# A sorted graph aggregation: broadcasts in halves, upper counts on two engines beside the decoding, low parts of the features by TensorE, and a folded 16-bit maximum

## The chip, the cores and the metric

The kernel runs on one core of a Trainium2 chip. The metric is the device time of one execution in microseconds (us). The engines are named as in the profile: PE (TensorE, matmuls; PEld its weight loads), DVE (VectorE), ACT (ScalarE), POOL (GpSimd) and SP (SyncE, which here only issues transfers). Each engine works through its own queue in order; semaphores tie the queues together.

## What is computed

The reference is one layer of a graph network with mean aggregation over 800,000 random edges between 12,500 nodes with 64 features each:

```python
N, deg, D = 12500, 64, 64
E = N * deg
nsum = _segment_sum(x[src], dst, N)
h_neigh = nsum * deg_inv[:, None]
return x @ w_self + h_neigh @ w_neigh
```

The sum over the edges of a node is the expensive part. The kernel doesn't gather a row of `x` per edge. It sorts the edges, and then does the gather and the sum with one-hot matrices on TensorE.

## The kernel before, in words

**Keys and sort.** Every edge becomes one 32-bit key: destination block (of 160 nodes, 78 of them), source block (of 128 nodes, 98 of them), and the low bits of both. A pair of blocks is a *bucket*; there are 7,644, of up to 128 edges each. Each of the 128 partitions sorts 6,250 edges by a comb sort on DVE (`sort_runs`, L227); elements without a partner in a stage are copied by ACT (L229). A list scheduler lays `prepare` and `self_terms` in between, by its own model of the engines. `prepare` finds the largest absolute value of `x` (ACT writes the absolute values to `y`, DVE reduces them, L527), makes a power-of-two scale `scl` from it, and splits the scaled features into two fp16 halves: `xh[:, :, 0]` is the rounded value (ACT, L550), `y` the difference (DVE, L551), `xh[:, :, 1]` 2048 times that (ACT, L552). It also counts, with two sign passes on ACT, whether any value is in a forbidden range.

**Two parts.** From `after_sort` on the order is as written (`manual_schedule`). Runs of the sorted rows are found, gathered across partitions by POOL (`gather_runs`: indirect DMAs `u<-d`, each followed by one or two `pad` memsets as a pause, L391, L304), and merged by DVE with min and max steps (`merge_runs`, L413, L453; ACT copies the unpaired elements, L418). Part 0 holds the first 4,736 buckets, part 1 the others. For each of the buckets a row of part 0 has (37), its start is found by counting: a pass over a window with an accumulator (`count_below`, L597 on ACT, L599 on DVE), a conversion to an address (`ix`, L622 on ACT), and an indirect DMA on POOL that fetches the window (`v<-d`, L603). The first 18 counts lie inside the merge; the 19 *upper counts* need its end. `decode_buckets` then takes ten groups of four windows: four DVE steps (L640 to L645), two narrowing copies on ACT, a store of the source bits to `sl` in DRAM by SP, four transposes on PE, and a copy into `dlT`. At its end it picks out leftover edges that fit no bucket (`e`, `top`).

**Part 1 while part 0 is summed.** The part-1 merge is a generator (`merge`). Its first 20 steps, block (0,2), are interleaved with the decoding; the next 20 and the others come a few per tile in the main loop, at `PACE` ns of work per tile, with a pause until tile `RESUME`. The part-1 gathers are split too: 64 of the 128 are issued during the part-0 merge, 32 (`FIRST` to `THEN`) behind the last `v` gather, and 32 (the list `runs`) one on every odd tile.

**Main loop.** `nodes` goes through 956 tiles of eight buckets. `one_hots` makes, for every 28 buckets, `ohs` (DVE, L821) from a broadcast of `sl` over all partitions (`slb`, issued by SP, L819, three buffers), and `ohd` (DVE, L824) from `dlT`. `gather` does eight matmuls `ct` (L850) which pick rows of `xh`, and copies them to fp16 `xg` (ACT L860, from tile 503 on every other one on DVE). `sums`, two to three tiles later, does sixteen matmuls into `acc` (L905). I call a tile's turn in `sums` its *job*. The leftover edges come in by 140 further gathers `lx` on POOL (L869), each with two matmuls in `sums` (L885). `uses` gives each one a due bucket: no earlier than its buckets are done, and for part 0 no earlier than a line in its number; the gather is issued 160 buckets (20 tiles) ahead of that, PE uses it when the job reaches it. All POOL gathers stand in one queue, in the order in which this loop writes them.

Of the kernel before, what the change touches and what calls it, by code (L numbers as in the profile page):

```python
# [11 lines left out]
F32 = mybir.dt.float32  # L12
BF = mybir.dt.bfloat16
FH = mybir.dt.float16
# [50 lines left out]
LOWER = 2240  # L65
LAST = 20
LAG = 4
OCT = 6
LEAST = 2 * HN * NDB
LEND = 14  # L70
# [71 lines left out]
    return c >= 128 + SHARED or c % 2 == 0  # L142


def on_act2(part):

    return part == 0


def constants():  # L150
    thr = bid_base(np.concatenate([BASE[p] + np.arange(ROWS[p]) * KPRS[p] for p in range(2)]))
    assert thr[-1] == 0x7F000000 and thr[-2] < TAIL
    thr[-1] = TAIL
    act = np.array([on_act(c) for c in range(NC1)])
    t1 = np.where(act, -(thr - 1).view(np.float32), thr.view(np.float32))
    mul = np.where(act, -1.0, 2.0)
    add = np.array([(n if a else 0) + lo - 1 for (lo, n), a in zip(WIN.w1, act)])
    add[128:] -= UPPER1
    assert max(lo + 2 * n for lo, n in WIN.w1[:128]) + WIDE[0] <= SPLITS[1]
    assert min(lo for lo, _ in WIN.w1[128:]) > UPPER1  # L160
    c1 = np.zeros((128, 3, NC1), np.float32)
    c1[:, 0], c1[:, 1], c1[:, 2] = t1, mul, add
    out = {"c1": c1}
    for p in range(2):
        kpr = KPRS[p]
        b = BASE[p] + np.arange(128)[:, None] * kpr + np.arange(kpr)[None]
        v = bid_base(np.minimum(b, NBID))
        act = np.array([on_act2(p) for k in range(kpr)])
        first = np.array([lo + (n / 2 + 0.25 if a else 0) for (lo, n), a in zip(WIN.w2[p], act)])
        mid = v | np.uint32(1 << 14)  # L170
        c2 = out[f"c2_{p}"] = np.zeros((128, 6, kpr), np.float32)
        c2[:, 0] = v.view(np.float32)
        c2[:, 1] = mid.view(np.float32)
        c2[:, 2] = -(mid - 1).view(np.float32)
        c2[:, 3] = np.where(act, -0.5, 1.0)
        at = [home(p, k) for k in range(kpr)]
        c2[:, 4] = first + np.arange(128)[:, None] * np.array(PITCH2)[at] - np.where(np.array(at) == 1, UPPER2 + SIDE, 0)
        c2[0::2, 5, 0] = c2[1::2, 5, 1] = 1.0
    return out
# [79 lines left out]
class Kernel:  # L259
# [242 lines left out]
    def prepare(self, xp, mps):  # L502

        nc = self.nc
        full = NB - 1
        tail = N - full * 128
        self.w2s = xp.tile([128, 2, D], F32, name="w2s")
        nc.gpsimd.memset(self.w2s, 0.0)  # L510
        for h in range(2):
            nc.sync.dma_start(self.wn[h * D:(h + 1) * D], self.I["w_neigh"])
            nc.sync.dma_start(self.w2s[h * D:(h + 1) * D, h], self.I["w_self"])
        x = self.x = xp.tile([128, NB, D], F32, name="x")
        nc.gpsimd.memset(x[:, full], 0.0)
        nc.sync.dma_start(x[:, :full], self.I["x"][:full * 128].rearrange("(b p) f -> p b f", p=128))
        nc.sync.dma_start(x[:tail, full], self.I["x"][full * 128:])
        dg = xp.tile([128, 128], F32, name="dg")
        nc.gpsimd.memset(dg, 0.0)
        fd = N // FB  # L520
        nc.sync.dma_start(dg[:fd, :FB], self.I["deg_inv"][:fd * FB].rearrange("(b p) -> b p", p=FB))
        nc.sync.dma_start(dg[fd:fd + 1, :N - fd * FB], self.I["deg_inv"][fd * FB:].unsqueeze(0))

        y = xp.tile([128, NB, D], F32, name="y")
        nc.scalar.activation(y, x, AF.Abs)
        m = xp.tile([128, 1], F32, name="m")
        nc.vector.tensor_reduce(m, y.rearrange("p b f -> p (b f)"), axis=mybir.AxisListType.X, op=OP.max)  # L527
# [23 lines left out]
        nc.vector.scalar_tensor_tensor(y, x, scl[:, :1], self.xh[:, :, 0], op0=OP.mult, op1=OP.subtract)  # L551
        nc.scalar.activation(self.xh[:, :, 1], y, AF.Copy, scale=2048.0)  # L552
        nc.sync.dma_start(self.xt.rearrange("(b p) f -> p b f", p=128), self.xh.rearrange("p b a f -> p b (a f)"))

        nc.scalar.activation(y, x, AF.Abs, scale=scl[:, :1])
        z = xp.tile([128, NB, D], BF, name="z")
# [31 lines left out]
    def count_below(self, part, k, acc):  # L588
# [2 lines left out]
        c2 = self.c2[part]  # L591
        lo, n = WIN.w2[part][k]
        w = view(self.rows, EDGE + lo, [[1, n]])
        on = on_act2(part)
        junk = self.keep.tile([128, max(n for _, n in WIN.w2[0] + WIN.w2[1])], BF, name=f"junk2{part}")
# [17 lines left out]
    def find_and_gather(self, part, ks, lag):  # L613


        scale = -0.5 if on_act2(part) else 1.0
        for i in range(len(ks) + lag):
            if i < len(ks):
                self.count_below(part, ks[i], self.acc2)
            if i >= lag:  # L620
                k = ks[i - lag]
                self.nc.scalar.activation(self.ix2[:, k:k + 1], self.acc2[:, k:k + 1], AF.Relu, scale=scale,  # L622
                                          bias=self.c2[part][:, 4, k:k + 1])
                self.gather_window(part, k, self.ix2)
            yield i
# [167 lines left out]
    def uses(self):  # L793
# [3 lines left out]
        for o in range(0, NBID, OCT * NB):  # L797
            end = min(o + OCT * NB, NBID)
            here = []
            for p in range(2):  # L800
                for c in range(64):
                    lo = max(o, BASE[p] + c * 2 * KPRS[p])
                    hi = min(end, BASE[p] + (c + 1) * 2 * KPRS[p])
                    if hi > lo:
                        here.append([max(hi + 56, 260 + 32 * c) if p == 0 else hi + 56, p, c, lo // NB, (hi - 1) // NB])
            at = end + 8
            for use in sorted(here)[::-1]:
                at = use[0] = min(use[0], at - 24)
# [3 lines left out]
    def one_hots(self, pool):  # L812
# [2 lines left out]
        nc = self.nc  # L815
        for c in range(0, NBID, 28):
            b = pool.tile([128, 28 * 128], BF, name="slb", bufs=3)
            src = self.sl[c:c + 28]
            nc.sync.dma_start(b, bass.AP(tensor=src.tensor, offset=src.offset, ap=[[0, 128], [1, 28 * 128]]))  # L819
            s = pool.tile([128, 28, 128], FH, name="ohs", bufs=3)  # L820
            nc.vector.tensor_scalar(s.rearrange("p c s -> p (c s)"), b, self.pidx[:, :1], None, op0=OP.is_equal)  # L821
            d = pool.tile([128, 14, HN, 2], FH, name="ohd", bufs=5)
# [286 lines left out]
    def sums_and_merge(self, es, mps, aps, u1, other, l2, l2b, l2a, va, vp):  # L1109
        tc = self.tc  # L1110
        vb = ExitStack()
        for _ in self.find_and_gather(0, range(NLOWER, KPRS[0]), 1):
            pass
        self.gather_runs(1, u1, range(FIRST, THEN))
        runs = list(range(THEN, 128))
        l2a.close()
        merge = self.merge_runs(1, u1, other, ((0, 2), (2, 1), (3, 1)))
        per = steps = 4 * len(MERGE[1][0])
        t, early = 0, per
        for k in self.decode_buckets(0, self.v, vp, mps):  # L1120
            t += 2800
            while t > 0 and early and k < KPRS[0]:
                t -= next(merge)
                early -= 1
        for _ in range(early):
            next(merge)
        va.close()

        self.fin = fin = es.enter_context(tc.tile_pool(name="fin", bufs=1, side="right"))
# [73 lines left out]
```

## Time and profile before

| | us |
|---|---|
| runs: median (lowest, highest of 3) | 1899.85 (1891.56, 1901.67) |
| the profiled execution | 1899.66 |
| its span in the trace | 1897.9 |
| DVE busy | 1672.6 (88%) |
| ACT busy | 1176.5 (62%) |
| PE busy (weight loads) | 972.7 (841.7) |
| POOL busy | 809.3 (43%) |
| DMA queue of SP and ACT (q1), share of 16 engines | 41.2% |

The stages on the profile's clock: keys until 46, sort and `prepare` until about 280, finding and gathering part 0 until about 551, merging it until 747, decoding until 811, leftovers until 821, first one-hot at 826, main loop to the end. A table of engines' busy time over all of the span mixes these stages; the rows to read are those of one stage, and the waits in it.

### The profile page before, as it was taken

How to read it: one execution, taken by the hardware profiler on the slowest of the kernel's cores; microseconds unless marked ns; L12 is line 12 of the kernel's file. 1: busy time of each engine (PE TensorE's matmuls, PEld its weight loads, DVE VectorE, ACT ScalarE, POOL GpSimd, SP SyncE). 2: the span in 40 equal slices, each digit the busy share in tenths (PEclk: the TensorE clock that was granted, in tenths of full speed). 3: DMA queues.
4: the chain of work that ended last, by engine and by line, in shares of the span. 5: the costliest groups of instructions: out<-in, count | busy, mean ns of one | idle time of the engine just before them, and what ended most of it. 6: DMA issues, size and time to landing. Idle time of an engine off the chain costs nothing.

```text
span 1897.9 us, 54529 instructions
## 1 busy us (share of the span) xinstructions
PE 972.7 (51%) x23659; PEld 841.7 (44%) x23659; DVE 1672.6 (88%) x1760; ACT 1176.5 (62%) x1853; POOL 809.3 (43%) x917
## 2 busy tenths in 40 slices
PE   0043000000000000039888888898879989998997
PEld 0033000000000000038777777787768877787886
DVE  7999999997749998779699999999799888788885
ACT  7463019205510022549888898898968878777886
POOL 1000000699889984898521331326554123322431
PEclk9995555555555555569999999999989999999999
DMA  4322000001100012257677877889768887888884
GB/s 152 70 68 68 0 32 0 26 20 52 22 20 10 10 40 66 58 190 279 207 240 245 244 256 257 245 267 322 234 206 283 285 255 263 242 266 265 273 259 139
DMA packets 104804, 305.24 MB, mean 161 GB/s; under 512 B 52945, under 2 KB 60491, under 8 KB 103915
## 3 DMA queue, kind: packets, MB, share of 16 engines
q1 hardware_dynamic: 86347, 277.44, 41.2%
q0 software_dynamic: 17632, 22.17, 8.6%
q8 instruction: 187, 3.06, 0.6%
q10 hardware_dynamic: 576, 2.07, 0.3%
q14 instruction: 62, 0.51, 0.1%
HBM read 282.20 MB, written 19.41 MB: 159 GB/s over the span
## 4 chain that ended last, share of the span: by engine, by line
DVE 43%; PE 23%; POOL 16%; issue 11%; DMA 3%; ACT 3%; DVEq 0%; SPq 0%; POOLq 0%; ACTq 0%
DVE u L453 15%; PE ct L850 13%; POOL u L391 12%; PE acc L905 9%; DVE a L227 7%; DVE b L227 7%; DVE ohd L824 6%; DVE ohs L821 4%; POOL pad L304 2%; POOL v L603 1%; ACT xg L860 1%; DMA slb<-sl 1%; PE po L968 1%; DVE u L413 1%; POOL lx L869 1%
## 5 line engine op out<-in xcount | busy, mean ns | idle before, releaser
L860 ACT ACTIVATE xg<-ct 128x1024 f16<-128x1024 f32 (+1 forms) x898 | 853.3, 1032 | 166.8 <-PE ct L850 135.3
L850 PE MATMUL ct<-xh,ohs 128*128 128x128 f16 x7644 | 543.1, 223 | 64.3 <-DVE ohs L821 27.3
L850 PEld LDWEIGHTS <-ohs 128*128 128x128 f16 x7644 | 449.0, 100 | 107.7 <-issue 57.5
L391 POOL DMA_INDIRECT u<-d,ix x256 | 362.2, 1415 | 217.1 <-DVE ix L383 175.4
L905 PE MATMUL acc<-ohd,xg 64*128 64x80 f16 x15288 | 405.5, 199 | 72.8 <-issue 49.1
L453 DVE TENSOR_TENSOR u<-u 128x1456 f32<-128x1456 f32 (+46 forms) x292 | 393.7, 1377 | 21.6 <-issue 14.6
L905 PEld LDWEIGHTS <-xg 64*128 64x128 f16 x15288 | 318.6, 96 | 144.6 <-issue 70.4
L824 DVE TENSOR_TENSOR ohd<-iota,dlT 128x2240 f16<-128x2240 bf16 x273 | 360.2, 1319 | 0.0
L869 POOL DMA_INDIRECT lx<-xt,lsrc x140 | 236.8, 1691 | 263.2 <-PE acc L885 224.4
L821 DVE TENSOR_SCALAR ohs<-slb,pidx 128x3584 f16<-128x3584 bf16 x273 | 315.0, 1154 | 34.4 <-PE ct L850 21.7
L381 PE MATMUL stp<-idf,st 128*128 128x128 f32 x2 | 0.9, 447 | 356.8 <-DVE st L379 356.8
L227 DVE TENSOR_TENSOR a<-b 128x608 f32<-128x608 f32 (+44 forms) x124 | 174.0, 1445 | 4.6
L227 DVE TENSOR_TENSOR b<-a 128x608 f32<-128x608 f32 (+44 forms) x124 | 173.9, 1444 | 4.3
L976 POOL DMA_DIRECT2D out<-o x25 | 23.6, 946 | 354.7 <-DVE o L975 288.4
L381 PEld LDWEIGHTS stp<-idf,st 128*128 128x128 f32 x2 | 0.4, 182 | 357.3 <-issue 357.3
L660 PE MATMUL tr<-idb,l 128*128 128x128 bf16 x60 | 8.2, 278 | 285.2 <-issue 240.9
L858 DVE CAST xg<-ct 128x1024 f16<-128x1024 f32 x64 | 78.3, 1224 | 70.2 <-PE ct L850 69.5
L660 PEld LDWEIGHTS <-l 128*128 128x128 bf16 x60 | 5.0, 119 | 288.2 <-issue 244.3
L418 ACT ACTIVATE u<-u 128x30 f32<-128x30 f32 (+34 forms) x136 | 29.8, 268 | 143.6 <-DVE u L453 74.5
L229 ACT ACTIVATE b<-a 128x1 f32<-128x1 f32 (+21 forms) x52 | 18.7, 383 | 135.3 <-DVE a L227 130.2
L597 ACT ACTIVATE junk<-u,c 128x166 bf16<-128x166 f32 (+36 forms) x37 | 26.7, 722 | 119.1 <-DVE u L453 119.0
L603 POOL DMA_INDIRECT v<-d,ix x60 | 77.8, 1297 | 47.5 <-ACT ix L622 35.0
(153 smaller groups left out, 868.7 us busy)
## 6 DMA issues: line engine op xcount, KB each, us to landing
slb<-sl SPq DMA_DIRECT2D x273, 896.0 KB
u<-d,ix POOLq DMA_INDIRECT x256
xt<-xh SPq DMA_DIRECT2D x1, 3136.0 KB
fo<-own SPq DMA_DIRECT2D x26, 120.0 KB
own<-os SPq DMA_DIRECT2D x12, 256.0 KB
out<-o POOLq DMA_DIRECT2D x24, 120.0 KB
lx<-xt,lsrc POOLq DMA_INDIRECT x140
rd<-dst SPq DMA_DIRECT2D x4, 521.0 KB
```

The costliest lines, as they stand in the source:

```text
L227: nc.vector.tensor_tensor(view(dst, lo + sh, [[st, g], [1, l]]), x, y, op=op)
L304: self.nc.gpsimd.memset(self.pad, 0.0)
L391: nc.gpsimd.indirect_dma_start(out=u[:nr, EDGE + p * w:EDGE + (p + 1) * w], out_offset=None, in_=src, in_offset=bass.IndirectOffsetOnAxis( ...
L453: nc.vector.tensor_tensor(view(dst, EDGE + o + out, d), view(src, EDGE + o + x, d), view(src, EDGE + o + x + gap, d), op=op)
L603: self.nc.gpsimd.indirect_dma_start(out=self.v[:, k].bitcast(F32), out_offset=None, in_=flat(self.d2[home(part, k)], 128 * PITCH2[home(par ...
L821: nc.vector.tensor_scalar(s.rearrange("p c s -> p (c s)"), b, self.pidx[:, :1], None, op0=OP.is_equal)
L824: nc.vector.tensor_tensor(d, self.iota[:, None].to_broadcast([128, 14, HN, 2]), ix, op=OP.is_equal)
L850: nc.tensor.matmul(ct[:, i * 128:(i + 1) * 128], cols[i][0], self.xh[:, (b0 + i) % NB].rearrange("p a f -> p (a f)"), start=True, stop=True)
L858: nc.vector.tensor_copy(xg[:, :cnt * 128], ct[:, :cnt * 128])
L860: nc.scalar.activation(xg[:, :cnt * 128], ct[:, :cnt * 128], AF.Copy)
L869: nc.gpsimd.indirect_dma_start(out=x, out_offset=None, in_=self.xt, in_offset=bass.IndirectOffsetOnAxis(ap=self.left[p][1][:, c:c + 1], ax ...
L905: nc.tensor.matmul(acc[h][:, db % OCT * HN:(db % OCT + 1) * HN], xg[r, i * 128:(i + 1) * 128], d[r], start=db % OCT == 0 and sb == 0, stop ...
```

## The change

Four edits, and one that goes with them.

1. `one_hots` issues the broadcast of 28 buckets as two transfers of 14 (448 KB each) into the two halves of the same buffer. The one-hot still runs over all 28.
2. `prepare`: the absolute values are written as bf16 (`z`), folded by four element-wise maxima down to 392 columns, and reduced from there. The low half is made on PE: for every eight blocks, `x` times a diagonal of the scale (fp32), minus the rounded half times an identity (fp16), summed in PSUM (`low`), from where ACT writes 2048 times it to `xh`. DVE's reduction of 6,272 elements and its pass at L551 go.
3. The upper counts of part 0 alternate between ACT and DVE (`on_act2(part, k)`), and the loop that decodes runs beside them, in slots that are budgeted at `SLOT` ns each. Only as many steps of the part-1 merge as fit in the budget are put there, five by the listing; the others follow in the main loop. The address conversion trails the count by two slots and not one.
4. The line below which a part-0 leftover gather isn't due is 380 + 24 c and not 260 + 32 c.

```diff
-def on_act2(part):
-    return part == 0
+def on_act2(part, k):
+    return part == 0 and (k < NLOWER or (k - NLOWER) % 2 == 0)
...
         y = xp.tile([128, NB, D], F32, name="y")
-        nc.scalar.activation(y, x, AF.Abs)
+        z = xp.tile([128, NB, D], BF, name="z")
+        nc.scalar.activation(z, x, AF.Abs)
+        most, n = z.rearrange("p b f -> p (b f)"), NB * D
+        fold = xp.tile([128, n // 2], BF, name="fold")
+        while n > 512:
+            n //= 2
+            nc.vector.tensor_tensor(fold[:, :n], most[:, :n], most[:, n:2 * n], op=OP.max)
+            most = fold
         m = xp.tile([128, 1], F32, name="m")
-        nc.vector.tensor_reduce(m, y.rearrange("p b f -> p (b f)"), axis=mybir.AxisListType.X, op=OP.max)
+        nc.vector.tensor_reduce(m, fold[:, :n], axis=mybir.AxisListType.X, op=OP.max)
...
-        nc.vector.scalar_tensor_tensor(y, x, scl[:, :1], self.xh[:, :, 0], op0=OP.mult, op1=OP.subtract)
-        nc.scalar.activation(self.xh[:, :, 1], y, AF.Copy, scale=2048.0)
+        by = xp.tile([128, 128], F32, name="by")
+        nc.scalar.activation(by, self.idf, AF.Copy, scale=scl[:, :1])
+        less = xp.tile([128, 128], FH, name="less")
+        nc.scalar.activation(less, self.idf, AF.Copy, scale=-1.0)
+        for b0 in range(0, NB, 8):
+            nb = min(8, NB - b0)
+            ps = mps.tile([128, 8, D], F32, name="low", tag="ct", bufs=3)
+            nc.tensor.matmul(ps[:, :nb], by, x[:, b0:b0 + nb], start=True, stop=False)
+            nc.tensor.matmul(ps[:, :nb], less, self.xh[:, b0:b0 + nb, 0], start=False, stop=True)
+            nc.scalar.activation(self.xh[:, b0:b0 + nb, 1], ps[:, :nb], AF.Copy, scale=2048.0)
...
-                        here.append([max(hi + 56, 260 + 32 * c) if p == 0 else hi + 56, p, c, lo // NB, (hi - 1) // NB])
+                        here.append([max(hi + 56, 380 + 24 * c) if p == 0 else hi + 56, p, c, lo // NB, (hi - 1) // NB])
...
-            src = self.sl[c:c + 28]
-            nc.sync.dma_start(b, bass.AP(tensor=src.tensor, offset=src.offset, ap=[[0, 128], [1, 28 * 128]]))
+            for j in range(0, 28, 14):
+                src = self.sl[c + j:c + j + 14]
+                nc.sync.dma_start(b[:, j * 128:(j + 14) * 128],
+                                  bass.AP(tensor=src.tensor, offset=src.offset, ap=[[0, 128], [1, 14 * 128]]))
...
     def sums_and_merge(self, es, mps, aps, u1, other, l2, l2b, l2a, va, vp):
-        for _ in self.find_and_gather(0, range(NLOWER, KPRS[0]), 1):
-            pass
-        self.gather_runs(1, u1, range(FIRST, THEN))
-        runs = list(range(THEN, 128))
-        l2a.close()
-        merge = self.merge_runs(1, u1, other, ((0, 2), (2, 1), (3, 1)))
-        per = steps = 4 * len(MERGE[1][0])
-        t, early = 0, per
-        for k in self.decode_buckets(0, self.v, vp, mps):
-            t += 2800
-            while t > 0 and early and k < KPRS[0]:
-                t -= next(merge)
-                early -= 1
-        for _ in range(early):
-            next(merge)
+        runs = list(range(THEN, 128))
+        merge = self.merge_runs(1, u1, other, ((0, 2), (2, 1), (3, 1)))
+        per = 4 * len(MERGE[1][0])
+        t, steps = 0, 0
+        ways = self.find_and_gather(0, range(NLOWER, KPRS[0]), 2)
+        decode = self.decode_buckets(0, self.v, vp, mps)
+        at = []
+        for k in range(3, KPRS[0] + 3, 4):
+            at.append(max(2 * len(at), at[-1] + 2 if at else 0, READY + min(k, KPRS[0] - 1) - NLOWER if k >= NLOWER else 0))
+        for slot in range(at[-1] + 2):
+            t += SLOT
+            if ways and next(ways, None) is None:
+                ways = None
+                self.gather_runs(1, u1, range(FIRST, THEN))
+            if slot < KPRS[0] - NLOWER and not on_act2(0, NLOWER + slot):
+                t -= 750
+            if slot in at or slot - 1 in at:
+                next(decode)
+                t -= 1175
+            while t > 0 and steps < per:
+                t -= next(merge)
+                steps += 1
+        for _ in decode:
+            pass
+        l2a.close()
```

What this does to the order of the queues, at the two places the prediction speaks of. First DVE, just behind the part-0 merge. `v` is decoded in groups of four steps; L413 and L453 are steps of the part-1 merge. Before:

```order
L640 TENSOR_TENSOR v<-v,c_0_67 128x4x128
L642 TENSOR_SCALAR w,cnt<-v 128x512
L644 TENSOR_SCALAR w<-v 128x512
L645 TENSOR_SCALAR v<-v 128x4x128
L413 TENSOR_TENSOR u<-u 128x2x16x41 x2
L453 TENSOR_TENSOR u<-u 128x2x655
L453 TENSOR_TENSOR u<-u 128x2x603
L640 TENSOR_TENSOR v<-v,c_0_67 128x4x128
L642 TENSOR_SCALAR w,cnt<-v 128x512
L644 TENSOR_SCALAR w<-v 128x512
L645 TENSOR_SCALAR v<-v 128x4x128
L453 TENSOR_TENSOR u<-u 128x2x650
```

And after, where L615 is a count on DVE, L656 to L661 the decoding, L415 and L455 the merge:

```order
L656 TENSOR_TENSOR v<-v,c_0_67 128x4x128
L658 TENSOR_SCALAR w,cnt<-v 128x512
L660 TENSOR_SCALAR w<-v 128x512
L661 TENSOR_SCALAR v<-v 128x4x128
L415 TENSOR_TENSOR u<-u 128x2x16x41
L615 TENSOR_SCALAR junk_1992,acc_0_1861<-u,c_0_67 128x566
L656 TENSOR_TENSOR v<-v,c_0_67 128x4x128
L658 TENSOR_SCALAR w,cnt<-v 128x512
L660 TENSOR_SCALAR w<-v 128x512
L661 TENSOR_SCALAR v<-v 128x4x128
L615 TENSOR_SCALAR junk_2014,acc_0_1861<-u,c_0_67 128x591
```

Between two groups of decoding there stood merge steps; now there stands a count, and all but the first merge step have moved back.

Second POOL, at the first leftover gather `lx`, among the part-1 run gathers `u`. Before, 39 of the last 64 `u` stand ahead of it:

```order
L391 DMA u<-d_1_61,ix_1468 128x48
L304 MEMSET pad 128x95 x2
L869 DMA lx<-xt,lsrc_2756 128x128
L391 DMA u<-d_1_61,ix_1468 128x48
L304 MEMSET pad 128x95 x2
L391 DMA u<-d_1_61,ix_1468 128x48
L304 MEMSET pad 128x95 x2
L869 DMA lx<-xt,lsrc_2756 128x128
```

After, 47 of the 64:

```order
L393 DMA u<-d_1_61,ix_1527 128x48
L306 MEMSET pad 128x95 x2
L887 DMA lx<-xt,lsrc_2791 128x128
L393 DMA u<-d_1_61,ix_1527 128x48
L306 MEMSET pad 128x95 x2
L887 DMA lx<-xt,lsrc_2791 128x128
L393 DMA u<-d_1_61,ix_1527 128x48
L306 MEMSET pad 128x95 x2
L393 DMA u<-d_1_61,ix_1527 128x48
L306 MEMSET pad 128x95 x2
L887 DMA lx<-xt,lsrc_2791 128x128
```

The first `lx` has moved eight `u` back, and the next ones stand closer together; by the eighth, 60 `u` are ahead of it and 59 were.

More of the change, by code (lines that the diff above doesn't have):

```diff
@@ L67 @@
 LAG = 4
+READY = 8
+SLOT = 1250
 OCT = 6
@@ L167, in constants @@
         v = bid_base(np.minimum(b, NBID))
-        act = np.array([on_act2(p) for k in range(kpr)])
+        act = np.array([on_act2(p, k) for k in range(kpr)])
         first = np.array([lo + (n / 2 + 0.25 if a else 0) for (lo, n), a in zip(WIN.w2[p], act)])
@@ L550, in prepare @@
         nc.scalar.activation(self.xh[:, :, 0], x, AF.Copy, scale=scl[:, :1])
-        nc.vector.scalar_tensor_tensor(y, x, scl[:, :1], self.xh[:, :, 0], op0=OP.mult, op1=OP.subtract)
-        nc.scalar.activation(self.xh[:, :, 1], y, AF.Copy, scale=2048.0)
+        by = xp.tile([128, 128], F32, name="by")
[8 more added lines that the diff above has]
+            nc.scalar.activation(self.xh[:, b0:b0 + nb, 1], ps[:, :nb], AF.Copy, scale=2048.0)
         nc.sync.dma_start(self.xt.rearrange("(b p) f -> p b f", p=128), self.xh.rearrange("p b a f -> p b (a f)"))
         nc.scalar.activation(y, x, AF.Abs, scale=scl[:, :1])
-        z = xp.tile([128, NB, D], BF, name="z")
         s = [xp.tile([128, 1], F32, name=f"s{i}") for i in range(2)]
@@ L593, in count_below @@
         w = view(self.rows, EDGE + lo, [[1, n]])
-        on = on_act2(part)
-        junk = self.keep.tile([128, max(n for _, n in WIN.w2[0] + WIN.w2[1])], BF, name=f"junk2{part}")
+        on = on_act2(part, k)
+        junk = self.keep.tile([128, max(n for _, n in WIN.w2[0] + WIN.w2[1])], BF, name=f"junk2{int(on)}")
         if on:
@@ L613, in find_and_gather @@
     def find_and_gather(self, part, ks, lag):
-        scale = -0.5 if on_act2(part) else 1.0
         for i in range(len(ks) + lag):
@@ L621, in find_and_gather @@
                 k = ks[i - lag]
-                self.nc.scalar.activation(self.ix2[:, k:k + 1], self.acc2[:, k:k + 1], AF.Relu, scale=scale,
+                self.nc.scalar.activation(self.ix2[:, k:k + 1], self.acc2[:, k:k + 1], AF.Relu,
+                                          scale=-0.5 if on_act2(part, k) else 1.0,
                                           bias=self.c2[part][:, 4, k:k + 1])
```

## The prediction

> **What bounds the kernel now.** I read the page's chain of work first, then the busy times in windows around the change, then the waits and the chain inside them.
>
> ```profile
> DVE 43%; PE 23%; POOL 16%; issue 11%; DMA 3%; ACT 3%; DVEq 0%; SPq 0%; POOLq 0%; ACTq 0%
> ```
> ```profile
> 747.00:811.00 64.00, 4.87 (x32) 2.76 (x32) 47.42 (x71) 39.20 (x100) 49.28 (x66) 0.50 0.25 73
> 811.00:827.00 16.00, 0.90 (x5) 0.45 (x5) 10.88 (x22) 1.88 (x5) 14.25 (x25) 0.50 0.34 116
> 827.00:926.00 99.00, 81.25 (x1905) 69.82 (x1906) 77.91 (x105) 77.87 (x101) 85.48 (x129) 0.88 0.73 260
> 926.00:1250.00 324.00, 278.10 (x7104) 241.77 (x7101) 320.81 (x301) 281.95 (x338) 86.91 (x48) 0.97 0.78 243
> ```
>
> The windows give the busy us of PE, weight loads, DVE, ACT and POOL, then granted clock, DMA share and GB/s. I call 747.1 us T0: the merge of part 0 ends there, and the upper counts begin. From 926 to 1250 DVE is full (320.8 of 324), so what counts is when that stretch can begin. Between T0 and 926 DVE idles 16.6 + 5.1 + 21.1 = 42.8 us, which is all that can be won behind T0. POOL is nearly full in the same time, and the waits say who is late:
>
> ```profile
> PE acc L885 <- DMA lx<-xt,lsrc: 3.2, 1, 3.2
> ```
> ```profile
> DVE ohs L821 <- PE ct L850: 11.7, 8, 5.6
> DVE u L413 <- DMA u<-d,ix: 8.1, 2, 4.2
> ```
> ```profile
> 901.25 6.10 DMA lx<-xt,lsrc
> 907.40 0.45 PE acc L885 x2
> ```
>
> These are PE's and DVE's waits of 826 to 960 (us, times, longest) and two steps of the chain (start, us). PE stands at the sixth left-over gather `lx` (#5, counted from 0) until 907.40; that gather began at 901.25, behind POOL's `u` gathers; DVE waits for PE (11.7 us) and twice for a `u` (8.1 us). So up to about 920 it is POOL's queue, one gather behind the other, that paces the end of this stage. What POOL's queue costs:
>
> ```profile
> L391 POOL DMA_INDIRECT u<-d,ix x59 | 80.3, 1360 | 10.4 <-issue 10.4
> L304 POOL MEMSET pad<- 128x95 f32 x118 | 28.3, 239 | 3.4
> L869 POOL DMA_INDIRECT lx<-xt,lsrc x8 | 9.7, 1209 | 3.2 <-issue 2.2 <-ACT xg L860 1.0
> ```
> ```profile
> 905.32 0.95 POOL L391 DMA_INDIRECT u<-d,ix  x1 [0.16 <-issue]
> 906.28 0.43 POOL L304 MEMSET pad<- 128x95 f32 x2
> 906.86 0.95 POOL L391 DMA_INDIRECT u<-d,ix  x1 [0.15 <-issue]
> ```
> ```profile
> 913.96 1.37 POOL L869 DMA_INDIRECT lx<-xt,lsrc  x1 [0.53 <-issue]
> ```
> ```profile
> 919.71 0.23 PE L885 MATMUL acc<-ohl,lx 128*128 128x80 f16 x2
> ```
>
> In 780 to 914 one `u` with its two pads takes (80.3 + 10.4 + 28.3 + 3.4)/59 = 2.08 us, one `lx` 12.9/8 = 1.61. Where DVE stood idle, at 905 to 907, a `u` took only 906.86 - 905.32 = 1.54. From the end of #7's gather (915.33) to its use at 919.71 pass 4.4 us, from #5's (901.25 + 1.55) 4.6: that is a landing.
>
> **The change, part by part.**
>
> *Prepare (beside the sort).* Groups of 46 to 282, and the first two one-hots:
>
> ```profile
> L551 DVE SCALAR_TENSOR_TENSOR y<-x,scl,xh 128x6272 f32<-128x6272 f32 x1 | 6.7, 6745 | 0.0
> L527 DVE TENSOR_REDUCE m<-y 128x1 f32<-128x6272 f32 x1 | 6.7, 6676 | 0.0
> L227 DVE TENSOR_TENSOR a<-b 128x2994 f32<-128x2994 f32 x2 | 6.5, 3277 | 0.1
> ...
> L555 ACT ACTIVATE y<-x,scl 128x6272 f32<-128x6272 f32 x1 | 5.5, 5532 | 0.0
> L576 PE MATMUL xt<-idf,x 128*128 128x128 f32 x49 | 13.2, 421 | 0.0
> ```
> ```profile
> 826.42 1.15 DVE L821 TENSOR_SCALAR ohs<-slb,pidx 128x3584 f16<-128x3584 bf16 x1 [5.01 <-DMA slb<-sl]
> 827.49 1.32 DVE L824 TENSOR_TENSOR ohd<-iota,dlT 128x2240 f16<-128x2240 bf16 x1
> ```
>
> The two long DVE steps go: 6.75 + 6.68 = 13.4 us. Four folds of 3136, 1568, 784 and 392 elements and a reduction of 392 come. No bf16 maximum is in the trace; at the f32 rate (3.28 us for 2994) they cost at most 6.9 + 0.5 us, at half of it some 4. I take 4.2, by the nearest row with half-width numbers, the one-hot's (2240 elements in 1.32 us; 5880 in 3.5, and the rest): a net 9.2 us less DVE. But the scale now waits for a longer chain, and the 5.5-us steps on ACT (the absolute value, two signs, `xh`) slide to later, shorter sort stages, whose edge copies also stand in ACT's queue; DVE waits for those. One such copy behind one 5.5-us step costs up to 5.5 us. TensorE's 13 chunks cost about 4 x 0.42 us each for the f32 part, and ACT 13 evacuations of 512 elements, on engines that idle there. I take 6 us lost of the 9.2 (bounds 0 and 10): T0 comes **3 us** earlier (bounds 9 earlier and 1 later).
>
> *Upper counts beside decoding.* DVE before (lines of 747 to 830):
>
> ```profile
> L453 DVE TENSOR_TENSOR u<-u 128x1040 f32<-128x1040 f32 (+18 forms) x19 | 23.4, 1263 | 15.2 <-issue 14.6
> ...
> L413 DVE TENSOR_TENSOR u<-u 128x1312 f32<-128x1312 f32 x2 | 4.7, 2428 | 0.0
> ```
> ```profile
> L599 DVE TENSOR_SCALAR_CACHE_REDUCE junk<-u,c x23: 332/642/805, 1275.0 to 1336.4; 128x114 bf16<-128x114 f32 x1, 128x180 bf16<-128x180 f32 x1, 128x220 bf16<-128x220 f32 x1, 128x251 bf16<-128x251 f32 x1
> ```
>
> Before, DVE stands 14.6 us behind ACT's 19 counts, and the first one-hot runs at 826.42, T0+79.3. Its work up to there is 47.4 + 10.9 = 58.3 us, of which 28.1 are merge steps, so 30.2 decoding. After, nine counts come (554 to 747 elements; 0.8 us was the largest of the 23 counts of part 1; I take 0.9, so 8 us) and five merge steps stay (two at 2.43, three at about 1.4: 9 us). 30.2 + 8 + 9 = 47, some 5 us of short waits, and 5.0 us for the first broadcast: first one-hot at **T0+57**, 22 us earlier against T0. Fifteen merge steps, some 19 us, go among the tiles, where DVE's idle 21.1 us takes them; by the order they are made up by about tile 90.
>
> But POOL gains nothing of this. Its last `v` gather now follows the last count, about T0+37 by the slots (before, the `u` began at 780.5, T0+33.4). Then the queue is as long as before: in it #7 stands behind 60 `u` instead of 59. Twelve `u` in the lighter time up to T0+57 at 1.75 (between 1.54 and 2.08), 45 or 48 more at 2.08. #5: 37 + 21 + 45 x 2.08 + 5 x 1.61 + 1.6 + 4.6 = **T0+166**, for job 63. #7: 37 + 21 + 48 x 2.08 + 7 x 1.61 + 1.4 + 4.4 = **T0+175**, for job 72.
>
> *The first `lx` fall due later* (jobs 48, 51, 54, 57, 60, 63, 69, 72 instead of 33, 37, 41, 45, 54, 63, 69, 72). PE's own pace:
>
> ```profile
> L885 PE MATMUL acc<-ohl,lx x22: 199/233/341, 875.0 to 951.4; 128*128 128x160 f16 x12, 128*128 128x80 f16 x10
> ```
>
> Job 33 used #0 at 875.0, job 72 used #7 at 919.71: 1.15 us a job, so job 48 was at about 892, T0+145. Shifted by 22 that is T0+123. #0 now lands at 37 + 21 + 35 x 2.08 + 6 = T0+137: PE stands there 14 us, and from there on each `lx` takes POOL longer (1 or 2 `u` and itself, 3.7 to 5.8 us) than three jobs take PE (3.4). The earlier start is eaten by #0 to #5.
>
> From #5 to job 72 it took 907.40 to 919.71, 12.3 us for nine jobs, because PE had cooled:
>
> ```profile
> 908.49 1.82 PE ct L850 x16
> 910.31 1.18 PE acc L905 x32
> ...
> 914.00 1.00 PE ct L850 x16
> ```
> ```profile
> 905.00:912.00 7.00, 4.60 (x72) 3.93 (x73) 2.39 (x2) 2.81 (x3) 5.58 (x11) 0.60 0.40 131
> ```
>
> The same 16 matmuls take 1.82 us just behind the wait and 1.00 six us later; the granted clock of 905 to 912 is 0.60. So job 72 falls on T0+166 + 12.3 = **T0+178**, against T0+172.6 before: 5 us later. The Trainium skill, TensorE: Matmul & The Clock Gate, Part 1, says that after one idle window of about 3.4 us the array runs at half clock until it has been busy for as long. By that rule the waits for #0 to #5, where each is that long, would keep PE at half clock, and the nine jobs would take 9 x (1.82 + 1.18)/2 = 13.5 us and not 12.3: an estimate with job 72 another us later. The trace agrees so far as one wait of 3.2 us went with a clock of 0.60.
>
> *Broadcasts in halves.* 273 more transfers in SP's queue; each one-hot waits for both.
>
> ```profile
> SPq L819 <- DVE ohs L821: 819.5, 254, 10.0
> ```
> ```profile
> DVE ohs L821 <- DMA slb<-sl: 9.9, 4, 5.0
> ```
>
> SP waits 819.5/254 = 3.2 us per broadcast for a free buffer, and DVE only 9.9 us in all for the data. I cost it at nothing while the extra is below 3.2 us per broadcast; it can win no more than those 9.9 us, and what it costs without that cover is in the last rival. The Trainium skill, SBUF — State Buffer, The DMA setup-cost knee, speaks against it: each transfer carries a fixed 2 us or so, and one should coalesce. Taken in series that would be an estimated 273 x 2 = 546 us, but under this cover 0; no run so far shows halves.
>
> **Sum.** The profiled execution took 1899.66 us, within 0.2 of the median of 1899.85. -3 (T0), +5 (job 72 against T0), and nothing for the fifteen merge steps, for the broadcasts and for the rest, where DVE's work is the same: 1899.7 - 3 + 5 = **1902 us**.
>
> **Rivals.** *Faster: POOL is no limit.* For it: a `u` beside an idle DVE takes 1.54. While PE stands at #0, DVE's buffers fill and it idles too, so POOL may speed itself up. At 1.75 throughout, #5 lands at 37 + 57 x 1.75 + 14.2 = T0+151, and job 72 comes at T0+163: 10 us earlier, 13 with T0's 3 and 19 if the sort gives all 9, so 1881 to 1887. At 1.54, PE's own pace decides, job 72 at T0+123 + 24 x 1.15 = T0+151, and the time is 1870 to 1875. It decides where a `u` costs below about 1.9. Against it: the 2.08 was measured with DVE busy 78% of the time.
>
> *Slower: more merging beside the gathers.* In the pure merge a `u` costs more:
>
> ```profile
> L391 POOL DMA_INDIRECT u<-d,ix x40 | 76.9, 1923 | 6.2 <-issue 6.2
> L304 POOL MEMSET pad<- 128x95 f32 x79 | 14.6, 185 | 2.3
> ```
>
> That is 100/40 = 2.5 us (600 to 700). Fifteen merge steps now lie beside the 48 `u`. At 2.3, #5 lands 10 us later, T0+176, job 72 at T0+188: 1899.7 - 3 + 15.4 = 1912, and 1916 if T0 comes 1 us later. It decides from about 2.25 us. Against it: the steps are spread thin.
>
> *The change does not bring what it says:* the sort loses to ACT all it gains, or halves come later than one whole: each us above the 3.2 costs up to 273 us; a few us over a few early broadcasts give 1905 to 1912.
>
> **Chances.** This kernel's measurement can tell about 0.5%, 9.5 us. My case (POOL eats the start; T0 by its bounds and 0.1 us more or less for a `u` make it 1892 to 1911) has 0.45: 0.35 of it within 0.5%, 0.04 faster, 0.06 slower. The faster rival has 0.34, the slower 0.16, the last 0.05 (slower). So 0.38 faster, 0.35 same, 0.27 slower. The range goes from 1874 to 1916: it leaves out the lowest end of the faster rival, and what lies above the slower one.
>
> **What would show it.** Right: the first one-hot near T0+57, a PE wait for `lx` above 10 us in all from job 48 on, `u` near 2.08, job 72 later than T0+172. Wrong: job 72 before T0+165 with no long `lx` wait; T0 later than 748 or earlier than 739; DVE waits for `slb` well above 10 us.

## The result, and the profile after

The changed kernel takes 1912.61 us (median of 6 runs, 1909.42 to 1915.5) against 1900.12 before (6 runs, 1891.56 to 1903.95): 1.0056 of before, 95% interval 1.0033 to 1.008. It is a little slower, by more than the interval leaves open. The profiled execution took 1911.18 us, with a span of 1909.4.

First the stretch that the forecast was about. Windows of the changed kernel from the end of the part-0 merge (742.9, the new T0) on; columns as before:

```profile
742.90:780.00 37.10, 4.86 (x32) 2.75 (x32) 32.74 (x63) 27.56 (x67) 20.41 (x19) 0.50 0.36 111
780.00:802.90 22.90, 0.90 (x5) 0.45 (x5) 14.90 (x32) 3.28 (x8) 20.03 (x38) 0.50 0.30 88
802.90:923.00 120.10, 76.82 (x1774) 66.71 (x1774) 87.19 (x109) 72.80 (x99) 105.28 (x157) 0.78 0.62 200
923.00:1250.00 327.00, 280.18 (x7263) 243.20 (x7265) 325.59 (x310) 290.92 (x354) 93.49 (x55) 0.99 0.80 246
```

The decoding is short now: DVE has 32.7 of 37.1 us to do, and the first one-hot runs at 802.9, 60.0 us behind T0 and not 79.3. But the stretch from there to 923 is 120 us long where it was 99, DVE idles 33 us in it, and only POOL is nearly full (105.3 us). From 923 on DVE is full again. PE's and DVE's waits up to 960, and two rows of PE and two of POOL on the timeline:

```profile
PE acc L903 <- DMA lx<-xt,lsrc: 35.5, 5, 25.5
```
```profile
DVE ohl L895 <- PE acc L903: 20.1, 1, 20.1
DVE ohs L839 <- PE ct L868: 11.8, 3, 8.8
```
```profile
886.05 0.32 PE L903 MATMUL acc<-ohl,lx 128*128 128x80 f16 x2 [25.47 <-DMA lx<-xt,lsrc]
...
923.32 0.23 PE L903 MATMUL acc<-ohl,lx 128*128 128x80 f16 x2 [0.59 <-DMA lx<-xt,lsrc]
```
```profile
780.87 0.94 POOL L393 DMA_INDIRECT u<-d,ix  x1 [0.30 <-issue]
```
```profile
882.52 0.95 POOL L887 DMA_INDIRECT lx<-xt,lsrc  x1 [0.96 <-issue]
```
```profile
L393 POOL DMA_INDIRECT u<-d,ix x63 | 91.2, 1447 | 11.1 <-issue 11.1
L306 POOL MEMSET pad<- 128x95 f32 x124 | 26.9, 217 | 3.6
```

PE's 3.2 us of waiting for `lx` have become 35.5, of which 25.5 at once: it reached job 48 about 860.6 and stood until 886.05, because POOL came to that gather only at 882.52, behind 47 `u`. DVE then stood 20.1 us behind PE. A `u` cost (91.2 + 11.1 + 26.9 + 3.6)/63 = 2.11 us. Job 72 used #7 at 923.3; before it was 919.7. So 19 us of earlier start against T0, and 4 us of earlier T0, were gone by job 72.

What the forecast did not have lies behind that. By the starts of the jobs in the two traces, the changed kernel is 2.1 us earlier than before at job 240 and 0.7 earlier at job 400, but 1.8 later at job 600 and 10.9 later at the last. So it had made up its 3.6 us and more by job 240, and then lost 13, most of it in the last third, where of the edits only the halves act.

### The profile page after: what moved, and what is told of

Its sections match the earlier page's. It is cut to its first block, busy times and chain, and to the rows that moved or that the text cites. A ratio compares the mean times of both kernels' runs of the same rounds, so it can differ in the third digit from the quotient of the medians.

```text
span 1909.4 us, 55011 instructions
## 1 busy us (share of the span) xinstructions
PE 979.7 (51%) x23698; PEld 843.2 (44%) x23698; DVE 1670.4 (87%) x1781; ACT 1171.1 (61%) x1849; POOL 799.7 (42%) x917
## 3 DMA queue, kind: packets, MB, share of 16 engines
q1 hardware_dynamic: 125659, 277.45, 44.1%
q8 instruction: 187, 3.06, 0.6%
## 4 chain that ended last, share of the span: by engine, by line
DVE 39%; PE 25%; POOL 16%; issue 11%; DMA 4%; ACT 3%; DVEq 0%; SPq 0%; ACTq 0%; POOLq 0%
DVE u L455 14%; PE ct L868 13%; POOL u L393 13%; PE acc L923 10%; DVE a L229 6%; DVE b L229 6%; DVE ohd L842 5%; DVE ohs L839 4%; POOL pad L306 3%; DMA slb<-sl 1%; ACT xg L878 1%; DVE u L415 1%; PE po L986 1%; DMA rd<-dst 1%; PE pw L598 1%
## 5 line engine op out<-in xcount | busy, mean ns | idle before, releaser
L393 POOL DMA_INDIRECT u<-d,ix x256 | 368.2, 1438 | 173.1 <-DVE ix L385 131.4
L923 PE MATMUL acc<-ohd,xg 64*128 64x80 f16 x15288 | 399.9, 199 | 56.2 <-issue 40.0
L455 DVE TENSOR_TENSOR u<-u 128x1456 f32<-128x1456 f32 (+46 forms) x292 | 394.2, 1377 | 7.2 <-ACT u L420 0.7
L887 POOL DMA_INDIRECT lx<-xt,lsrc x140 | 224.7, 1605 | 268.6 <-PE acc L903 234.6
L374 ACT ACTIVATE junka<-b,c 128x132 bf16<-128x132 f32 (+46 forms) x205 | 90.7, 442 | 11.8 <-DVE b L229 5.9
```

The costliest lines, as they stand in the source:

```text
L374: nc.scalar.activation(junks[0][:, :n], w, AF.Sign, bias=self.c1[:, 0, c:c + 1], accum_out=a)
L393: nc.gpsimd.indirect_dma_start(out=u[:nr, EDGE + p * w:EDGE + (p + 1) * w], out_offset=None, in_=src, in_offset=bass.IndirectOffsetOnAxis( ...
L455: nc.vector.tensor_tensor(view(dst, EDGE + o + out, d), view(src, EDGE + o + x, d), view(src, EDGE + o + x + gap, d), op=op)
L887: nc.gpsimd.indirect_dma_start(out=x, out_offset=None, in_=self.xt, in_offset=bass.IndirectOffsetOnAxis(ap=self.left[p][1][:, c:c + 1], ax ...
L923: nc.tensor.matmul(acc[h][:, db % OCT * HN:(db % OCT + 1) * HN], xg[r, i * 128:(i + 1) * 128], d[r], start=db % OCT == 0 and sb == 0, stop ...
```

## The experiments

All ratios are against the kernel before, measured beside it on the same chip, with their 95% intervals. They aren't the quotients of the medians that stand beside them (for e1_whole that would be 0.9965).

**1. Each part alone, and all but the halves.** Four kernels, measured together: `e1_whole` is the changed kernel with the old broadcast,

```diff
-            for j in range(0, 28, 14):
-                src = self.sl[c + j:c + j + 14]
-                nc.sync.dma_start(b[:, j * 128:(j + 14) * 128],
-                                  bass.AP(tensor=src.tensor, offset=src.offset, ap=[[0, 128], [1, 14 * 128]]))
+            src = self.sl[c:c + 28]
+            nc.sync.dma_start(b, bass.AP(tensor=src.tensor, offset=src.offset, ap=[[0, 128], [1, 28 * 128]]))
```

`e2_halves` is the kernel before with the reverse of that, `e3_prepare` is before with the new `prepare`, and `e4_counts` is before with the counts, the slots and the due line. Expected of them:

> The changed kernel with the broadcast of 28 buckets whole again; the other edits stay. In the changed kernel's trace job 600 begins 1.8 us later than before and the last job 10.9 later, so some 9 us are lost behind job 600, where neither the counts nor the prepare step act. Theory A (the halves cost these 9 us, by more packets beside the matmuls): 1900 to 1904 us. Rival B (the halves cost nothing; the late loss comes with the other edits, by where the late part falls): 1910 to 1914 us. Both: first one-hot near 803, one PE wait for lx of about 25 us near 886, job 600 near 1514.

> The kernel before with the halved broadcasts alone. Theory A (halves cost about 9 us behind job 600): 1907 to 1911 us, first one-hot within 2 us of 826, jobs to 600 as before. Rival B: 1898 to 1902 us.

> The kernel before with the new prepare alone (folded 16-bit maximum, low parts by TensorE). The changed kernel reached the end of the part-0 merge at 742.9 and before at 747.1, so the sort should end 4 us earlier here too, and all that follows with it: 1895 to 1897 us if nothing takes it up later (theory A and my prediction). Rival C (what the sort wins is lost again at the next wait, for POOL's gathers or late): 1899 to 1902 us.

> The kernel before with the counts on two engines beside the decoding, the merge steps moved and the later due line, without the halves and the new prepare. Theory A: first one-hot near 807 (T0 + 60), a PE wait of 25 us for the first lx, job 72 near 927, some 7 us later than before, of which 5 are lost for good or made up by job 600 (the changed kernel made up its 3.6 us by job 240): 1900 to 1906 us. Rival B (the late loss comes with this edit): 1910 to 1916 us. Rival D (POOL is no limit): below 1885 us.

| | ratio | interval | median us (before 1904.43) |
|---|---|---|---|
| e1_whole | 0.9939 | 0.9911 to 0.9967 | 1897.69 |
| e2_halves | 1.0077 | 1.0049 to 1.0105 | 1918.17 |
| e3_prepare | 0.9932 | 0.9904 to 0.9959 | 1892.02 |
| e4_counts | 0.9974 | 0.9948 to 0.9999 | 1899.78 |

Theory A holds in its main point: the halves cost 0.8% alone, more than the 9 us expected (0.0077 x 1904.4 = 14.7 us), and without them the changed kernel is 0.6% faster than before. Rivals B, C and D fall. But none of the four medians lies in the range that theory A gave: the halves cost more, and the other three kernels are faster than it said (e4_counts by 0.2 us). Nor do the jobs up to 600 come as before in e2_halves: in its trace job 600 is 15.9 us later (that execution took 1928.34 us, 10 above the median). The counts are worth 0.3%, with an interval that all but reaches zero. PE's waits from 780 to 960 in their trace (without halves and without the new prepare), and in that of e1_whole (without halves), show where the 20 us of earlier start went:

```profile
PE acc L887 <- DMA lx<-xt,lsrc: 37.9, 4, 26.5
```
```profile
PE acc L901 <- DMA lx<-xt,lsrc: 38.3, 4, 28.0
```

The new prepare gave more than expected: 0.7%, 13 us, with an interval of 8 to 18, where the trace shows T0 at 742.3 and not 747.1, 4.8 us. The rest, some 8 us, is not explained, and this trace can't explain it: the profiled execution took 1900.22 us, 8 above the median, and its last job begins 0.5 us later than before.

**2. What of the halves costs.** In the last third PE's waits marked "issue" stand out: idle time in which the engine waited for nothing that the profile shows. The rows of 1420 us to the end, of before, of e2_halves, and of the changed kernel:

```profile
PE acc L905 <- issue: 23.0, 26, 2.4
PE ct L850 <- issue: 14.8, 9, 3.2
```
```profile
PE acc L907 <- issue: 37.1, 29, 2.6
PE ct L852 <- issue: 18.9, 13, 2.6
```
```profile
PE acc L923 <- issue: 30.1, 26, 3.7
PE ct L868 <- issue: 14.1, 13, 2.0
```

37.8 us before, 56.0 with halves, 44.2 in the changed kernel. Gaps between matmuls of over 1 us from job 520 on are 17 with 28 us before, 26 with 47 us in e2_halves. Set beside the DMA packets, they are alike: from 1430 us to the end 26 of 27 such gaps of e2_halves, and 17 of 18 before, end 1.2 to 1.6 us after a packet of 16 KB of the instruction queue has landed (187 such packets in the whole run, 3.06 MB, which is 65 B for each of the 47,318 instructions of PE and its weight loads). So PE seems to wait for its program, and in this pair of traces for longer when the broadcasts come in halves. DVE, which waits for the broadcasts themselves, does so for 9.7 us in e2_halves and 9.9 before. The next three test this; two split the transfer otherwise, one takes half of the data away. Their edits:

```diff
+            for p in range(0, 128, 64):      # e5_rows
+                nc.sync.dma_start(b[p:p + 64], bass.AP(tensor=src.tensor, offset=src.offset, ap=[[0, 64], [1, 28 * 128]]))
...
+            for j in range(0, 28, 7):        # e6_quarters, with 7 in place of 14 in the transfer
...
-            nc.vector.tensor_scalar(s.rearrange("p c s -> p (c s)"), b, self.pidx[:, :1], None, op0=OP.is_equal)
+            nc.vector.tensor_scalar(s.rearrange("p (h c) s -> p h (c s)", h=2), b[:, None].to_broadcast([128, 2, 14 * 128]),
+                                    self.pidx[:, :1], None, op0=OP.is_equal)   # e7_less, b holds 14 buckets
```

> The kernel before with each broadcast in two transfers again, but of 64 partitions x 28 buckets each, so that a packet stays 7168 B (in the halves it was 3584 B). Halved by buckets it was 1.0077 of before. Theory A1 (it is the smaller packets: 0.170 us each and two for one of 0.314): 0.998 to 1.003 of before. Theory A2 (it is that there are two transfers): 1.005 to 1.010.

> The kernel before with each broadcast in four transfers of 7 buckets (packets of 1792 B). If the loss follows packets or transfers (A1 or A2) it grows with their number: 1.012 to 1.025 of before, with more and longer PE waits of over 1 us for nothing but 'issue' behind job 520 than the 26 (47 us) of the halves and the 17 (28 us) of before. Rival E (the loss of the halves was something else, such as where PE's program happens to lie): 0.997 to 1.010, with no trend.

> The kernel before with half of the broadcast data: only the first 14 of each 28 buckets are broadcast, and the one-hot is made of them twice, so the second half of each 28 buckets gets the wrong source rows. Theory A (PE's waits marked issue are waits for instruction packets, which come later the longer the broadcasts keep the DMA engines busy): waits over 1 us behind job 520 fall from 17 to below 8, and the time to 0.98 to 0.99 of before. Rival F (those waits have another cause, such as PE's own queue): as many waits as before, 0.996 to 1.003. If the one-hot on DVE gets slower by the repeated operand, the trace shows it at that line.

`e7_less` tells whether the broadcasts' bytes stand behind these waits, and they do, more than expected: 0.9668 (0.9598 to 0.9737), 1842.38 us. Its one-hots on DVE cost as before (median 1145 ns). The windows from 1420 to the end, of e7_less, and from 1432 of before:

```profile
1420.00:1842.00 422.00, 406.53 (x10873) 361.36 (x10870) 383.69 (x418) 372.03 (x412) 148.20 (x89) 0.99 0.56 149
```
```profile
1432.00:1898.00 466.00, 415.21 (x10722) 363.03 (x10714) 379.97 (x411) 368.83 (x404) 134.98 (x89) 0.98 0.79 252
```

PE is busy 96% of the time and was 89%. The gaps over 1 us from job 520 on fall from 17 to 1, and of the "issue" waits there is left:

```profile
PE ct L851 <- issue: 1.0, 1, 1.0
```

From job 520 to the last the same matmuls take 401.8 us where before took 455.7. Of these 54 us, 37 are the "issue" waits (37.8 to 1.0) and 16 are PE's busy time (412.7 to 396.8), which no experiment here explains. So in this kernel the bytes of the broadcasts are paid for by PE, for the larger part in waits that fit its instruction stream, and not by whoever reads the broadcast. The instruction packets themselves take as long in both (from job 520 on 1.04 us on average before, 1.09 in e7_less); if they come late, it is their start that is late, and that no trace here shows. How the halves add load: before, a broadcast packet of 7168 B takes 0.314 us on average (behind 1430 us), and with halves two packets take 2 x 0.170 = 0.340; the queue's share of the engines goes from 41.2 to 44.1% in the changed kernel (q1 of the two pages: packets, MB, share):

```profile
q1 hardware_dynamic: 86347, 277.44, 41.2%
```
```profile
q1 hardware_dynamic: 125659, 277.45, 44.1%
```

But that this added load is what the halves cost is not shown, and the quarters speak against it. `e6_quarters` came to 1.0034 (0.9996 to 1.0072) at a share of 46.0%, with 42.5 us of those waits and 19 gaps of over 1 us: less than the halves, where both A1 and A2 expected more. It lies in the range of rival E, that the halves lost by something else. Its interval overlaps that of the halves, so a step from halves to quarters is not measured, but a cost that grows with the number of packets, or with the load, is not supported. `e5_rows` told nothing of A1 and A2: it came to 1.1282 (1.1217 to 1.1346), because transfers to 64 partitions are slow in another way: their packets, 7168 B too, took 0.515 us and not 0.314, and the queue's share was 57.7%. It does say once more whom that hits: PE's waits for issue at the `acc` line rose to 175.8 us in the whole span, and were 49.1, while DVE's for the broadcasts rose from 9.9 to 24.2.

**3. Is it POOL's queue that takes the start?** `e8_nopad` is e1_whole without the pauses (two `pad` memsets of POOL) behind the part-1 run gathers from the 65th on:

```diff
-            self.pause(PAUSE[part])
+            self.pause(PAUSE[part] if p < FIRST or part == 0 else 0)
```

> The changed kernel with whole broadcasts (e1_whole, 0.9939 of before) and without the pauses behind the part-1 run gathers from the 65th on. A u then costs about 1.6 us of POOL instead of 2.11. My theory (POOL's queue takes what the earlier start gives): the first lx lands near T0+119 instead of T0+143, PE's wait for it falls from 25 us to below 8, job 72 comes some 15 to 20 us earlier, and the time is 0.984 to 0.989 of before. Rival G (DVE's work bounds this stretch anyway, or DVE pays for the missing pauses): 0.992 to 0.996, job 72 earlier but job 200 not.

0.9772 (0.9718 to 0.9825), 1864.7 us, six runs from 1858.25 to 1870.86. PE's wait for `lx` and POOL's `u` in 780 to 905:

```profile
PE acc L901 <- DMA lx<-xt,lsrc: 13.2, 3, 7.4
```
```profile
L393 POOL DMA_INDIRECT u<-d,ix x64 | 88.9, 1388 | 19.5 <-issue 19.5
```

A `u` costs 108.4/64 = 1.69 us. Job 72 begins at 899.3 where it was 926.2 in e1_whole, and the 27 us stay: job 200 is 34 us earlier, the last job 35. With POOL's queue shorter the earlier start is kept. So the theory holds, though not in its sizes: PE's wait fell to 13.2 us and not below 8, and yet 27 us were won by job 72 where I expected 15 to 20. Rival G falls for this program.

**4. The same without pauses, varied.** Then four variants, measured together on another chip: `e9_old_counts_nopad` is e3_prepare without pauses, `e10_nopad_halves` and `e11_nopad_quarters` are e8_nopad with split broadcasts, and `e12_lead` is e8_nopad with

```diff
-            ... uses[len(picked)][0] - 160 <= b0 ...
+            ... uses[len(picked)][0] - 240 <= b0 ...
```

> The kernel before with the new prepare (e3_prepare, 0.9932 of before) and without the pauses, so without the counts on two engines; e8_nopad, which has them too, came to 0.9772. Theory A (the earlier start is worth something only where POOL's queue is short): the first one-hot stays at T0+79, PE no longer waits for lx, job 72 comes at about T0+162 to 168, and the time is 0.985 to 0.992 of before, so that the counts are worth 8 to 15 us more without the pauses than with them (with the pauses they were worth 5 +- 5 us alone). Rival H (the pauses were the whole loss and the counts are worth nothing): 0.976 to 0.981.

> e8_nopad (0.9772) with the broadcasts in halves. If halves cost what they cost before (0.8 to 1.2%): 0.985 to 0.989 of before. Rival E (the cost was an accident of the two programs it was measured in): 0.974 to 0.980.

> e8_nopad (0.9772) with the broadcasts in quarters; on the kernel before, quarters came to 1.0034 (0.9996 to 1.0072), less than the halves' 1.0077, against a cost that grows with the number of transfers. If quarters truly cost less than halves: 0.978 to 0.984 here and below the halves of the same call. If the two are alike and the first difference was chance: within 0.004 of the halves.

> e8_nopad with the lx gathers issued 240 buckets ahead of their use, not 160. #0 then stands behind 42 of the 64 u instead of 47, so it lands about 5 x 1.7 = 8 us earlier. My theory: PE's waits for lx fall from 13 us to below 6, job 72 comes 3 to 7 us earlier, and the time is 0.972 to 0.976 of before. Rival G (DVE's work bounds the stretch by now): job 72 earlier, job 200 not, 0.976 to 0.979.

| | ratio | interval | median us (before 1909.2) |
|---|---|---|---|
| e9_old_counts_nopad | 0.9958 | 0.9932 to 0.9984 | 1900.62 |
| e10_nopad_halves | 0.9973 | 0.9937 to 1.001 | 1906.15 |
| e11_nopad_quarters | 0.9989 | 0.9961 to 1.0018 | 1905.96 |
| e12_lead | 0.9922 | 0.989 to 0.9953 | 1892.15 |

Their times fell outside what either theory had expected (that quarters lie within 0.004 of halves was one of the answers, but means little here). In e11_nopad_quarters and e12_lead what is missing against e8_nopad is gone by job 48: 25.7 of the 30.7 us at the last job, and 37.3 of 36.1. That has a cause of its own. In e12_lead PE's waits for `lx` are gone from its list, and job 48 still comes at 902.4. On its timeline, from 828 on ("remote" is a wait that ended by nothing the trace shows):

```profile
831.28 0.94 POOL L393 DMA_INDIRECT u<-d,ix  x1 [0.30 <-issue]
...
832.53 0.94 POOL L393 DMA_INDIRECT u<-d,ix  x1 [0.30 <-issue]
...
852.10 0.22 PE L921 MATMUL acc<-ohd,xg 64*128 64x80 f16 x1 [2.58 <-issue]
...
855.63 0.22 PE L921 MATMUL acc<-ohd,xg 64*128 64x80 f16 x1 [2.58 <-issue]
...
869.64 1.15 DVE L837 TENSOR_SCALAR ohs<-slb,pidx 128x3584 f16<-128x3584 bf16 x1 [39.48 <-remote]
869.70 1.02 ACT L876 ACTIVATE xg<-ct 128x1024 f16<-128x1024 f32 x1 [14.37 <-remote]
```

POOL's gathers run back to back, one each 1.25 us, and as long as they do, nearly nothing else runs: a matmul of 0.2 us about every 2 us, no one-hot for 39.5 us, no broadcast packet from 835 to 870 by the DMA records. It is not the load: from 835 to 865 the DMA engines were 12.9% busy, with the packets of POOL's gathers alone. It ends some 5 us behind the last `u` of the row. The other three have the same in part: DVE's longest "remote" wait between 800 and 960 is 16.9 us in e10_nopad_halves and 30.2 in e11_nopad_quarters, and ACT waits 13.4 us in all for "remote" in e9_old_counts_nopad; DVE's in the kernel before was 2.6, and the changed kernel and e8_nopad have none. In e8_nopad most gathers beside DVE's work took 1.3 to 1.6 us, and in the main loop at most six in a row were 1.25 us apart; the longest such rows are 11 in e9 and e10, 22 in e11 and 29 in e12. So the pauses seem to have a use, and taking them all away is a bet. What tips a program over isn't settled: e8_nopad ran on one chip and the four on another, and it was not run there. Nor can their times say what the counts or the halves are worth without pauses; a single pause, which might keep most of the 27 us, was not tried. The fastest version that does all of the work is e8_nopad, 0.9772.

What the halves cost can be read behind all this, from job 520 to the last, in the traces of all the kernels (one execution each):

| broadcasts | traces | us | PE busy | PE idle, "issue" |
|---|---|---|---|---|
| whole | before, e1, e3, e4, e8, e9, e12 | 447.7 to 461.8 (mean 455.4) | 407.2 to 417.9 (412.1) | 33.8 to 47.3 (38.8) |
| halves | after, e2, e10 | 469.7, 476.8, 467.2 | 418.3, 418.5, 414.1 | 47.6, 56.0, 46.2 |
| quarters | e6, e11 | 460.5, 458.2 | 414.5, 414.7 | 42.5, 38.4 |

In three different programs the halves lose some 16 us here, 11 of them in waits marked issue. So their cost isn't an accident of one program, and it lies in this stretch. The quarters lose 4, at the highest DMA load of all (0.85 to 0.86 of the engines' time, against 0.79 to 0.82 for the others in the table). Why halves cost and quarters hardly do stays open.

## Why the prediction was right, and where it was not

What I forecast of the early stage came out by its own steps, the place better than the sizes. The time did not: the step that failed is *Broadcasts in halves*, costed at nothing. That 1912.6 us lies in the range is luck: it is above the 1892 to 1911 of my own case, and meets the 1912 of the slower rival, whose condition (a `u` of 2.25 us or more) was not met. The direction was worth little too, since +2 us is far below the 9.5 that I said could be told, and I gave faster (0.38) a higher chance than slower (0.27).

- **Prepare.** Folds and reduction took 1.79 + 0.97 + 0.56 + 0.36 + 0.55 = 4.23 us (4.2 forecast). DVE's waits ahead of its sort steps rose over the whole span from 4.6 + 4.3 to 8.6 + 4.8 us, 4.5 lost (6 forecast). T0 came 4.2 us earlier (3 forecast). Right. That prepare alone came to 13 us and not 5 is open.
- **First one-hot** T0+60 (T0+57 forecast), first `u` of the batch T0+38 (T0+37). Right.
- **POOL eats the start.** `u` 2.11 us (2.08), first long wait 25.5 us (14), job 72 at T0+180.4 (T0+178) against T0+172.6 before. Right, and experiment 3 shows it by shortening the queue. The first wait was longer since PE came to job 48 at T0+118, 5 us earlier than I had shifted it, and the gather was there at T0+143, 6 us later. In the end two errors of opposite sign met: #5 was used at T0+169.7 (166), and from there to job 72 passed 10.8 us and not the 12.3 of before. The granted clock was 0.50 from 906.0 to 912.56, 0.51 up to 916.3, which is 3.7 us behind the wait for #5, and 1.00 from there to 923.3. The trace agrees with the Trainium skill, TensorE: Matmul & The Clock Gate, Part 1, that the array runs at half clock until it has been busy for a window of about 3.4 us. My 13.5 us for nine jobs, all at half clock, did not follow from that rule.
- **Broadcasts in halves**: 0 forecast, 14.7 us measured on the kernel before. I asked whether the data comes in time for DVE, and there it does: SP's slack covered it, and DVE waited 7.3 us for `slb` in the changed kernel and 9.9 before. I did not ask who else uses the DMA engines: PE's instruction packets do. In the place of nothing the runs show some 16 us behind job 520, 11 of them in PE's waits marked issue; why the quarters don't lose as much is open. The rule of the Trainium skill, SBUF — State Buffer, The DMA setup-cost knee, which I set aside because of that slack, pointed the right way, though its 2 us per transfer would be an estimated 546 us in series and the runs show 14.7, and quarters (819 more transfers) came to 1.0034 where halves came to 1.0077.
- **Sum.** 1902 forecast, 1912.6 measured. T0 and job 72 make +3.6 us in the two traces (+2 forecast); the rest is lost behind job 520, 14 us in these two traces, where all three kernels with halves lost. The parts measured alone, -13, -5 and +15 us (each 5 more or less), would make -3 and not +12.5, so they seem not to add. Beside the others the halves cost 1.2% (from 0.9939 to 1.0056, measured at two times) and alone 0.8%, but these intervals overlap.
- **Rivals.** The faster one fell at 2.11 us per `u`. In e8_nopad, at 1.69, what it described came about: job 72 at T0+158 (T0 is 741.1 there), between its 163 and 151. That kernel, which has no halves either, is faster than the rival's 1870 to 1887: 1864.7. The slower one fell: `u` did not reach 2.25. The last, that halves come later than one whole, had 0.05; the halves did cost, but not by coming late.

## What to carry to other kernels

A stage that starts earlier gains only if every queue that feeds it starts earlier too: look for the in-order queue that runs through the stage boundary (here POOL's gathers), and place its uses by its own pace. Slack at the reader of a transfer does not make the transfer free: ask who shares the DMA engines, PE's instruction stream first, and look for PE waits marked "issue". Change such things one at a time: here a gain of 0.6% and a loss of 0.8 to 1.2% were in one bundle.

## What the runs showed of the hardware

- PE's idle time marked "issue" late in the main loop depends on the bytes that the broadcasts move: with half of the broadcast bytes (DMA share 0.56 and not 0.79) gaps over 1 us fell from 17 to 1, and the kernel from 1903 to 1842 us. It fits waiting for instruction packets: 17 of 18 such gaps before end 1.2 to 1.6 us after a packet of 16 KB has landed.
- POOL's indirect gathers back to back, 1.25 us apart, went with PE, DVE, ACT and the broadcasts being held up for some 40 us (29 gathers in a row, e12_lead) while the DMA engines were only 12.9% busy; with two memsets of 0.2 us between them no "remote" wait of more than 4.9 us was seen.
- A broadcast in two transfers to 64 partitions each is slower per byte than one to 128: packets of the same 7168 B took 0.515 us and not 0.314, and the kernel 1.128 of before.
